# New ranks in a planned kernel, with diagonal blocks and conversion sums moved to DMA (gated attention and a low-rank mixer)

## Chip, cores, metric

One core of one Trainium2 chip. The metric is the device time of one execution, in microseconds; the median of several is quoted.

## The reference, cut

```python
# attention: B=4, H=8, S=768, D=48; a gate a = a_re + i a_im with |a| clipped to 0.999
S_re, S_im = a * S   (complex);  S_re += k v^T;  y_t = q_t . S_re        # step by step in t
x = y as (B, S, 384)
h = x^T @ U @ V              # mixes ALL 768 positions of a batch, rank 32
u = x + h^T
out = u + relu(u @ w_ch1) @ w_ch2        # 384 -> 1536 -> 384
```

The kernel cuts each sequence into chunks of 128 positions: 6 chunks a batch, 24 in all, numbered through. `x^T @ U` needs all six chunks of a batch, so the mixer of batch 0 can't start before chunk 5 has left attention.

## The kernel before

It doesn't write its instructions in program order. Every operation is declared with an engine, an estimated duration and a **rank**, and a list scheduler (`Plan.order`) simulates the engines and emits, on each free engine, the ready operation of the lowest rank. The result is one fixed order for each engine; on the chip each engine walks through its list and waits where an input is missing.

```python
# cut: the heart of Plan.order
while free[e] <= now and ready[e]:
    r = heapq.heappop(ready[e])        # lowest rank among the READY ones
    n = r[1]
    if not fits(n):                    # no free buffer: try the next
        kept.append(r)
        continue
    ...
    out.append(n)
    free[e] = now + ops[n][1]          # estimated duration
```

```python
# cut: ranks of the kernel before (i = chunk, lo = first chunk of a group of two)
#   gates lo-1.6   angles lo-1.5   prep i-0.8   levels i   rest i+0.5
#   conversion: w1 0.6 + 0.8*p (p = 0..5), UV 3.2, w2 7.0 + 0.2*f   mixing (up, down): 100+m
def single(p, rank, to, o, pieces):    # cut: float64 -> float32, seven VectorE instructions a piece
    ...
    DVE(two, rank, lambda: nc.vector.scalar_tensor_tensor(out=xf(), in0=lo(), scalar=2.0 ** -52, in1=xf(), op0=OP.mult, op1=OP.mult), ...)
    DVE(two, rank, lambda: nc.vector.tensor_tensor(out=o, in0=o, in1=xf(), op=OP.add), reads=[cx], writes=[to])

# cut: the second half of a group's gates ("turns"), with ScalarE's trigonometric table loaded
switch(R2, "trig_and_small")
ACT sign; ACT arctan; DVE y = ...; ACT y = y/pi + 1/4
for i in group:                        # the phase is summed from chunk to chunk
    if not first of its batch:
        POOL(... nc.gpsimd.dma_start(out=of(y, i)[0:1], in_=fo(i - 1)[CH - 1:CH], accum_op=OP.add) ...)
    PE ph = prefix^T @ y;  ACT F = round(ph);  DVE F = ph - F
ACT abs; ACT sin; ACT sin              # cs, which prep of both chunks needs

# cut: chain(i), the rest of it
for j in range(CH // BLK):
    ACT(0.4, RR, lambda js=js: nc.scalar.copy(out=get(*ATi)[js, :, js], in_=get(*DGi)[js]), [DGi], [ATi + (("d", js.start),)])
```

## Time and profile before

| | before |
|---|---|
| median of 3 runs | 816.72 us (814.86 to 817.06) |
| span of the profiled run | 815.9 us |
| first `mixed` matmul (end of stage 1) | 185.5 us |
| TensorE busy | 743.5 us |

Read it as two stages. Up to the first `mixed`, only attention can run. After it, the mixer's matmuls (`up`, `down`) fill every gap of TensorE. **Stage 1** goes from 10 us (the first matmul) to the first `mixed`; its length minus TensorE's busy time in it is its **idle**, and the same for stage 2. For the kernel before, the windows at this cut (columns: stretch, length, PE, PEld, DVE, ACT, POOL, clock, DMA share, GB/s) are:

```profile
10.00:185.50 175.50, 120.42 (x2032) 93.43 (x2032) 142.54 (x202) 132.31 (x261) 4.87 (x6) 0.75 0.40 98
185.50:815.90 630.40, 623.07 (x7480) 471.27 (x7480) 301.76 (x408) 330.57 (x713) 43.13 (x54) 0.99 0.15 34
```

So stage 1 has 175.5 - 120.4 = 55.1 us idle, and stage 2 has 7.3, the last store.

### The profile page before, as it was taken

The numbers are of one execution on the slowest core, as the hardware profiler recorded it, in microseconds if no ns is written. First come the engines' busy times: TensorE is split into PE (matmuls) and PEld (weight loads), VectorE is DVE, ScalarE is ACT, GpSimd is POOL, SyncE is SP. The second block draws the span as 40 slices with busy tenths as digits, with TensorE's granted clock in tenths as the row PEclk, the third lists the DMA queues.
The fourth block names the chain that finished last, engine by engine and source line by source line (L and its number), as shares of the span: only waits on it lengthen the run. The fifth ranks groups of instructions, "written<-read, shape, count | busy, mean of one in ns | idle before, by whom it ended". The sixth has DMA issues, their size and how long they took to land.

```text
span 815.9 us, 21434 instructions
## 1 busy us (share of the span) xinstructions
PE 743.5 (91%) x9512; PEld 564.7 (69%) x9512; DVE 447.2 (55%) x622; ACT 468.7 (57%) x983; POOL 55.9 (7%) x89
## 2 busy tenths in 40 slices
PE   2556786779999999999999999999999999999996
PEld 1445565657877877787787688687786867677683
DVE  3899687888978594747657585455451210110100
ACT  6886676877876787878587677745341312021120
POOL 3000000000101010010001010010000000000000
PEclk9767666898999999999999999999999999999999
DMA  7435323344022221403122240200000000000000
GB/s 186 113 91 132 90 41 99 60 117 107 13 59 51 50 53 38 90 12 58 42 47 47 47 90 2 49 22 1 21 12 10 11 10 10 10 10 19 10 10 20
DMA packets 131532, 40.11 MB, mean 49 GB/s; under 512 B 127088, under 2 KB 127984, under 8 KB 131440
## 3 DMA queue, kind: packets, MB, share of 16 engines
q1 hardware_dynamic: 129264, 33.99, 19.0%
q0 software_dynamic: 2176, 4.75, 1.7%
q8 instruction: 75, 1.23, 0.6%
q14 instruction: 17, 0.14, 0.1%
HBM read 33.59 MB, written 4.72 MB: 47 GB/s over the span
## 4 chain that ended last, share of the span: by engine, by line
PE 82%; DVE 6%; ACT 5%; issue 3%; DMA 3%; POOL 0%; POOLq 0%; ACTq 0%; DVEq 0%
PE up L765 23%; PE down L776 22%; PE tr L551 5%; PE inner L585 5%; PE tot L467 4%; PE dk L695 3%; PE yT L681 3%; PE es ps L450 3%; PE ph L511 2%; PE yT L685 2%; PE mixed L747 2%; PE ks ps L667 2%; DVE QK L248 2%; PE corners L632 2%; DMA y<-F 1%
## 5 line engine op out<-in xcount | busy, mean ns | idle before, releaser
L765 PE MATMUL up<-uT,w 128*128 128x256 f32 x864 | 201.8, 384 | 0.0
L776 PE MATMUL down<-w,h 128*128 128x384 f32 x576 | 199.6, 489 | 0.0
L248 DVE TENSOR_TENSOR QK<-QK,T 96x1024 f32<-96x1024 f32 (+1 forms) x144 | 172.8, 1206 | 24.0 <-PE corners L632 16.7
L765 PEld LDWEIGHTS up<-uT,w 128*128 128x128 f32 x864 | 159.2, 190 | 23.9 <-issue 1.4
L776 PEld LDWEIGHTS down<-w,h 128*128 128x128 f32 x576 | 105.0, 190 | 60.0 <-issue 0.4
L245 ACT ACTIVATE h<-up 128x256 f32<-128x256 f32 x144 | 55.2, 383 | 147.6 <-PE up L765 146.7
L551 PE MATMUL tr<-ident,qkc 128*96 128x128 f32 x384 | 58.5, 298 | 11.8 <-DVE qkc L248 10.8
L585 PEld LDWEIGHTS inner<-QK 96*32 96x32 f32 x4608 | 48.2, 112 | 28.6 <-issue 18.1
L251 DVE TENSOR_TENSOR xo<-down,xo 128x384 f32<-128x384 f32 x24 | 13.4, 556 | 97.4 <-PE down L776 97.0
L554 ACT COPY QK<-tr 96x512 f32<-96x512 f32 x96 | 52.8, 582 | 23.6 <-PE tr L551 22.7
L585 PE MATMUL inner<-QK 96*32 96x16 f32 (+1 forms) x4608 | 55.6, 192 | 11.1 <-DVE QK L248 10.7
L551 PEld LDWEIGHTS tr<-ident,qkc 128*96 128x96 f32 x384 | 44.5, 136 | 25.4 <-DVE qkc L248 13.6
L248 DVE TENSOR_TENSOR qkc<-qk,cs 128x768 f32<-128x768 f32 x48 | 44.1, 956 | 28.4 <-PE tr L551 21.9
L251 DVE TENSOR_TENSOR xo<-mixed,xo 128x384 f32<-128x384 f32 x24 | 13.3, 556 | 81.7 <-PE mixed L747 80.8
L467 PEld LDWEIGHTS tot<-total,ll 128*96 128x96 f32 x384 | 39.7, 180 | 8.6 <-ACT ll L462 3.1
L467 PE MATMUL tot<-total,ll 128*96 128x63 f32 x384 | 40.8, 263 | 2.5 <-ACT ll L462 2.5
L623 ACT COPY AT<-DG 32x256 f32<-32x256 f32 x96 | 38.4, 400 | 6.9 <-DVE DG L592 5.6
L681 PE MATMUL yT<-AT,VP 128*64 128x128 f32 x384 | 41.3, 305 | 0.9 <-ACT AT L651 0.5
L450 PE MATMUL es ps<-l,mid 128*128 128x384 f32 x48 | 24.4, 635 | 19.4 <-DVE l L440 19.4
L782 POOL DMA_DIRECT2D out_dram<-xo x24 | 13.6, 565 | 333.3 <-DVE xo L251 325.9
L712 ACT COPY xo<-yr 128x384 f32<-128x384 f32 x24 | 11.4, 476 | 43.0 <-DMA out_dram<-xo 39.2
L514 DVE SCALAR_TENSOR_TENSOR F<-F,ph 128x384 f32<-128x384 f32 x24 | 13.3, 554 | 41.1 <-ACT F L245 41.1
(92 smaller groups left out, 972.2 us busy)
## 6 DMA issues: line engine op xcount, KB each, us to landing
ar<-in_a_re_dram SPq DMA_DIRECT2D x24, 192.0 KB, 3.2
ai<-in_a_im_dram SPq DMA_DIRECT2D x24, 192.0 KB, 3.5
qk<-in_q_dram SPq DMA_DIRECT2D x24, 192.0 KB, 3.1
qk<-in_k_dram SPq DMA_DIRECT2D x24, 192.0 KB, 3.5
VP<-in_v_dram SPq DMA_DIRECT2D x24, 192.0 KB, 2.8
raw<-in_moe_w_ch_dram SPq DMA_DIRECT2D x6, 768.0 KB, 5.4
raw<-in_moe_w_ch_dram SPq DMA_DIRECT2D x12, 384.0 KB, 3.9
out_dram<-xo POOLq DMA_DIRECT2D x24, 192.0 KB, 2.2
```

What stands on the lines that cost most here:

```text
L245: return nc.scalar.activation(out=o, in_=i, func=f, **kw)
L248: nc.vector.tensor_tensor(out=o, in0=a, in1=b, op=OP.mult)
L251: nc.vector.tensor_tensor(out=o, in0=a, in1=b, op=OP.add)
L450: PE(0.65, R1, lambda: nc.tensor.matmul(out=get(*ps), lhsT=mid, rhs=of(l, i), start=True, stop=True), [l, ("mid", 0)], [ps, ("sums", g, i)])
L467: nc.tensor.matmul(out=get(*ps)[0:D2, h, 0:NTOT], lhsT=get(*ll)[:, h].rearrange("p u d -> p (u d)"), rhs=total, start=True, stop=True)
L551: nc.tensor.transpose(out=get(*ps)[0:D2, j], in_=get(*qkc)[:, u, hh * HH + j].rearrange("p u d -> p (u d)"), identity=ident)
L554: ACT(c_act(HH * CH) - 0.05, R1, lambda u=u, hh=hh, ps=ps: nc.scalar.copy(out=get(*QK)[:, u, hh * HH:(hh + 1) * HH], in_=get(*ps)[0:D2]), ...
L585: nc.tensor.matmul(out=get(*ps)[js, h], lhsT=k_of(h)[:, js], rhs=part(q_of(h)[:, js], "p"), start=True, stop=True, tile_position=(0, j * BLK))
L623: ACT(0.4, RR, lambda js=js: nc.scalar.copy(out=get(*ATi)[js, :, js], in_=get(*DGi)[js]), [DGi], [ATi + (("d", js.start),)])
L681: nc.tensor.matmul(out=a[u * DP:(u + 1) * DP, p], lhsT=vv[:, h], rhs=get(*ATi)[:, h], start=True, stop=(c == 0), tile_position=(0, u * DP))
L765: nc.tensor.matmul(out=get(*ps), lhsT=w1[:, f, ff * 128:(ff + 1) * 128], rhs=get(*uT)[:, f], start=(f == 0), stop=(f == KD - 1))
L776: nc.tensor.matmul(out=get(*ps), lhsT=get(*h)[:, ff, cc * CH:(cc + 1) * CH], rhs=w2[:, ff], start=(ff == 0), stop=(ff == KF - 1))
```

## The change

Its intent: let VectorE and ScalarE do less in stage 1 (the last sum of each conversion and the placing of the diagonal blocks go to DMA), and let nothing unurgent stand in attention's way (ranks, with constants that look searched for). The diff, cut to its core:

```diff
+PARAM = {"gates": -0.48, "angles": -1.91, "prep": -2.39, "levels": -4.96, "rest": 1.63, "w1": 18.64, "w2": 32.63, "first": 6.42}
+    def urgency(kind, n):
+        if kind == "load":
+            return n - 20
+        if kind in ("small", "mixing"):
+            return n + (1000 if kind == "mixing" else -1000)
+        if kind in ("w1", "w2"):
+            return PARAM[kind] + 0.01 * n
+        return n + PARAM[kind] + (PARAM["first"] if n >= NCH else 0)
 ...
-        DVE(two, rank, lambda: nc.vector.tensor_tensor(out=o, in0=o, in1=xf(), op=OP.add), reads=[cx], writes=[to])
+        POOL(1.0, rank, lambda: nc.gpsimd.dma_start(out=o, in_=xf(), accum_op=OP.add), reads=[cx], writes=[to], late=4.0)
 ...
-            ACT(0.4, RR, lambda js=js: nc.scalar.copy(out=get(*ATi)[js, :, js], in_=get(*DGi)[js]), [DGi], ...)
+            SP(0.15, RR, lambda js=js: nc.sync.dma_start(out=get(*ATi)[js, :, js], in_=get(*DGi)[js]), [DGi], ...)
 ...
+    AT_ONCE = (0, 1, 2, 3)      # groups (chunks 0 to 5) whose sines come in their own session
+        waits = [waves]         # the others: in the next group's trigonometric session
```

Also: `cx` has two buffers instead of one, T six instead of five, VP three instead of four, `qkc` is halved, the loads have ranks of their own, the scaled phase has its own tile `z` (it was `y`), the sign of the gate is taken before the trigonometric session and no longer in it, one table load of the first group goes, and the plan multiplies TensorE's durations in the first batch by 1.3.

More of the change, by code (lines that the diff above doesn't have):

```diff
@@ L23, with __init__ @@
 BLK = 32
+PARAM = {"gates": -0.48, "angles": -1.91, "prep": -2.39, "levels": -4.96, "rest": 1.63, "w1": 18.64, "w2": 32.63, "first": 6.42}
 class Plan:
-    def __init__(self, lag):
-        self.lag = lag
+    def __init__(self, lag, urgency):
+        self.lag, self.urgency = lag, urgency
         self.ops, self.log, self.tag, self.bufs = [], {}, {}, {}
@@ L55, in order @@
         ops = self.ops
+        rank = [self.urgency(*o[3]) for o in ops]
         left = [len(o[5]) for o in ops]
@@ L83, in order @@
             if not left[n]:
-                heapq.heappush(ready[o[0]], (o[3], n))
+                heapq.heappush(ready[o[0]], (rank[n], n))
         while True:
@@ L116, in order @@
                         if not left[m]:
-                            heapq.heappush(ready[ops[m][0]], (ops[m][3], m))
+                            heapq.heappush(ready[ops[m][0]], (rank[m], m))
         assert len(out) == len(ops), "the plan is stuck"
@@ L178 @@
     singles = pool("singles")
-    plan = Plan(0.06)
+    def urgency(kind, n):
[6 more added lines that the diff above has]
+        return n + PARAM[kind] + (PARAM["first"] if n >= NCH else 0)
+    plan = Plan(0.06, urgency)
     makers, T, pools = {}, {}, {}
@@ L218, in c_dma, with PE @@
         return n * 512 / 170e3
-    def PE(*a, **kw):
-        plan.add("PE", *a, **kw)
+    def PE(cost, rank, *a, **kw):
+        plan.add("PE", cost * (1.3 if rank[0] not in ("small", "mixing") and rank[1] < NCH else 1.0), rank, *a, **kw)
     def ACT(*a, **kw):
@@ L271 @@
     total = singles.tile([128, NTOT], FP, name="total")
+    F = singles.tile([128, GC, DM], FP, name="F")
     w1 = singles.tile([128, KD, FF], FP, name="w1")
@@ L288 @@
     AT, DG, VP = [], [], []
-    for n in range(4):
+    for n in range(3):
         VP.append(singles.tile([128, H, DP], FP, name="VP%d" % n))
@@ L298, in constants @@
     def constants():
-        SP(0.4, -7.5, lambda: nc.sync.dma_start(out=prefix, in_=spans[:, PRE * CH:(PRE + 1) * CH]), writes=[("prefix", 0)])
-        SP(0.6, -2.4, lambda: nc.sync.dma_start(out=mask, in_=masks), writes=[("mask", 0)])
+        SP(0.4, ("load", 0.1), lambda: nc.sync.dma_start(out=prefix, in_=spans[:, PRE * CH:(PRE + 1) * CH]), writes=[("prefix", 0)])
+        SP(0.6, ("load", 1.2), lambda: nc.sync.dma_start(out=mask, in_=masks), writes=[("mask", 0)])
         e = prefix.rearrange("p (b t) -> p b t", t=8)
-        POOL(0.5, -7, lambda: nc.gpsimd.tensor_tensor(
+        POOL(0.5, ("load", 0), lambda: nc.gpsimd.tensor_tensor(
             out=mid.rearrange("p (b t) -> p b t", t=8), in0=e[:, :, 3:4].to_broadcast([128, CH // 8, 8]), in1=e,
@@ L323, in totals @@
                     nc.gpsimd.tensor_tensor(out=to[:, 1:m], in0=ends[:, 1:m], in1=ends[:, 0:m - 1], op=OP.subtract)
-        POOL(2.5, -6, totals, reads=[("prefix", 0)], writes=[("total", 0)])
+        POOL(2.5, ("load", 1), totals, reads=[("prefix", 0)], writes=[("total", 0)])
         def pairs():
@@ L329, in pairs @@
                 nc.vector.tensor_tensor(out=mask[:, 5], in0=mask[:, 5], in1=mask[:, n], op=OP.bitwise_or)
-        DVE(0.5, -4, pairs, writes=[("mask", 0)])
+        DVE(0.5, ("load", 1), pairs, writes=[("mask", 0)])
     def load_a(g):
@@ L338, in load_a @@
             for i in range(lo, hi):
-                SP(c_dma(DM), lo - 8 if g == 0 else lo - 3, lambda nm=nm, src=src, i=i: nc.sync.dma_start(
+                SP(c_dma(DM), ("load", (0, 0.5, 3)[g] if g < 3 else lo + 3), lambda nm=nm, src=src, i=i: nc.sync.dma_start(
                     out=get(nm, g)[:, i - lo], in_=rows(src, i)), writes=[(nm, g, i)])
@@ L345, in load_qkv @@
         for u, src in enumerate((q, k)):
-            SP(c_dma(DM), i - 2.3, lambda u=u, src=src: nc.sync.dma_start(out=get("qk", i)[:, u], in_=rows(src, i)),
+            SP(c_dma(DM), ("load", (1.3, 2.5)[i] if i < 2 else i + 3.7), lambda u=u, src=src: nc.sync.dma_start(out=get("qk", i)[:, u], in_=rows(src, i)),
                writes=[("qk", i, u)])
-        SP(c_dma(DM), i - 2.0, lambda: nc.sync.dma_start(out=get("VP", i)[:, :, 0:D], in_=rows(v, i)), writes=[("VP", i)])
+        SP(c_dma(DM), ("load", (1.4, 2.6)[i] if i < 2 else i + 4), lambda: nc.sync.dma_start(out=get("VP", i)[:, :, 0:D], in_=rows(v, i)), writes=[("VP", i)])
     def single(p, rank, to, o, pieces):
@@ L359, in single @@
             for a, at in zip(pieces, ends):
-                SP(c_dma(a.shape[1]), rank - 1.5, lambda a=a, at=at: nc.sync.dma_start(out=o[:, at:at + a.shape[1]], in_=a),
+                SP(c_dma(a.shape[1]), ("load", 3.6 + p * 0.5), lambda a=a, at=at: nc.sync.dma_start(out=o[:, at:at + a.shape[1]], in_=a),
                    writes=[to])
@@ L363, in single @@
         buffer(("raw", p), "raw", 2, [128, WP, 2])
-        buffer(("cx", p), "cx", 1, [128, WP])
+        buffer(("cx", p), "cx", 2, [128, WP])
         for a, at in zip(pieces, ends):
-            SP(c_dma(2 * a.shape[1]), rank - 1.5, lambda a=a, at=at: nc.sync.dma_start(
+            SP(c_dma(2 * a.shape[1]), ("load", (1, 2, 3.5)[p] if p < 3 else 3.6 + p * 0.5), lambda a=a, at=at: nc.sync.dma_start(
                 out=get("raw", p)[:, at:at + a.shape[1]], in_=a.bitcast(U32).rearrange("p (m two) -> p m two", two=2)),
@@ L393, in weights @@
             for f in range(KD):
-                single(p, 0.6 + 0.8 * p, ("w1", f, h), w1[:, f, h:h + WP], [moe_w_ch1[f * 128:(f + 1) * 128, h:h + WP]])
+                single(p, ("w1", p), ("w1", f, h), w1[:, f, h:h + WP], [moe_w_ch1[f * 128:(f + 1) * 128, h:h + WP]])
                 p += 1
-        single(p, 3.2, ("UV", 0), UV, [moe_U[c * 128:(c + 1) * 128] for c in range(NCH)] +
+        single(p, ("w1", p), ("UV", 0), UV, [moe_U[c * 128:(c + 1) * 128] for c in range(NCH)] +
                [moe_V.rearrange("r (s m) -> (r s) m", m=m)])
@@ L399, in weights @@
         for n in range(NP):
-            SP(0.6, 3.2, lambda n=n: nc.sync.dma_start(out=V[n * R:(n + 1) * R].rearrange("r (s m) -> r s m", m=m),
+            SP(0.6, ("load", 7), lambda n=n: nc.sync.dma_start(out=V[n * R:(n + 1) * R].rearrange("r (s m) -> r s m", m=m),
                                                        in_=UV[:, NCH * R:]), reads=[("UV", 0)], writes=[("V", 0, n)])
         for f in range(0, KF, 2):
-            single(p, 7.0 + 0.2 * f, ("w2", f), w2[:, f:f + 2].rearrange("p f m -> p (f m)"),
+            single(p, ("w2", f), ("w2", f), w2[:, f:f + 2].rearrange("p f m -> p (f m)"),
                    [moe_w_ch2[e * 128:(e + 1) * 128] for e in (f, f + 1)])
@@ L412, in gates @@
         W = (hi - lo) * DM
-        R1, R2 = lo - 1.6, lo - 1.5
+        R1, R2 = ("gates", lo), ("angles", lo)
         ca, cd = c_act(W), c_dve(W)
-        x, y, l, n, ar, ai = names = [(nm, g) for nm in ("x", "y", "l", "n", "ar", "ai")]
-        for b in names[:4]:
-            buffer(b, "g" + b[0], 1, [128, GC * DM])
+        x, y, l, n, z, ar, ai = names = [(nm, g) for nm in ("x", "y", "l", "n", "z", "ar", "ai")]
         def t(b):
@@ L424, in of @@
             return get(*b)[:, (i - lo) * DM:(i - lo + 1) * DM]
-        ACT(ca, R1, lambda: act(t(x), t(ar), AF.Square), [ar], [x])
-        ACT(ca, R1, lambda: act(t(y), t(ai), AF.Square), [ai], [y])
-        DVE(cd, R1, lambda: add(t(x), t(x), t(y)), [y], [x])
-        DVE(c_one(W), R1, lambda: nc.vector.tensor_scalar(out=t(x), in0=t(x), scalar1=M2LO, scalar2=M2HI, op0=OP.max,
-                                                          op1=OP.min), [], [x])
-        switch(R1, "natural_log_exp_and_others")
@@ L432, in gates @@
-        ACT(ca, R1, lambda: act(t(n), t(ar), AF.Abs), [ar], [n])
-        table(ca, R1, lambda: act(t(l), t(x), AF.Ln), [x], [l])
-        table(ca, R1, lambda: act(t(x), t(l), AF.Exp, scale=0.5), [l], [x])
-        DVE(cd, R1, lambda: add(t(x), t(x), t(n)), [n], [x])
-        table(ca, R1, lambda: act(t(y), t(l), AF.Exp, scale=-0.5, bias=leps), [l], [y])
-        table(ca, R1, lambda: act(t(y), t(y), AF.Ln, bias=1.0), [], [y])
-        ACT(ca, R1, lambda: act(t(l), t(l), AF.Relu, scale=-0.5, bias=lmax), [], [l])
@@ L440, in gates, with magnitudes @@
-        DVE(cd, R1, lambda: nc.vector.scalar_tensor_tensor(out=t(l), in0=t(l), scalar=LNMAX, in1=t(y), op0=OP.subtract,
-                                                           op1=OP.add), [y], [l])
-        table(ca, R1, lambda: act(t(x), t(x), AF.Ln), [], [x])
-        table(ca, R1, lambda: act(t(x), t(x), AF.Exp, scale=-1.0), [], [x])
-        DVE(cd, R1, lambda: mul(t(x), t(x), t(ai)), [ai], [x])
+        def magnitudes():
+            for b in names[:4]:
+                buffer(b, "g" + b[0], 1, [128, GC * DM])
+            ACT(ca, R1, lambda: act(t(x), t(ar), AF.Square), [ar], [x])
+            ACT(ca, R1, lambda: act(t(y), t(ai), AF.Square), [ai], [y])
+            DVE(cd, R1, lambda: add(t(x), t(x), t(y)), [y], [x])
+            DVE(c_one(W), R1, lambda: nc.vector.tensor_scalar(out=t(x), in0=t(x), scalar1=M2LO, scalar2=M2HI, op0=OP.max,
+                                                              op1=OP.min), [], [x])
+            ACT(ca, R1, lambda: act(t(n), t(ar), AF.Abs), [ar], [n])
+            table(ca, R1, lambda: act(t(l), t(x), AF.Ln), [x], [l])
+            table(ca, R1, lambda: act(t(x), t(l), AF.Exp, scale=0.5), [l], [x])
+            DVE(cd, R1, lambda: add(t(x), t(x), t(n)), [n], [x])
+            table(ca, R1, lambda: act(t(y), t(l), AF.Exp, scale=-0.5, bias=leps), [l], [y])
+            table(ca, R1, lambda: act(t(y), t(y), AF.Ln, bias=1.0), [], [y])
+            ACT(ca, R1, lambda: act(t(l), t(l), AF.Relu, scale=-0.5, bias=lmax), [], [l])
+            DVE(cd, R1, lambda: nc.vector.scalar_tensor_tensor(out=t(l), in0=t(l), scalar=LNMAX, in1=t(y), op0=OP.subtract,
+                                                               op1=OP.add), [y], [l])
+            table(ca, R1, lambda: act(t(x), t(x), AF.Ln), [], [x])
+            table(ca, R1, lambda: act(t(x), t(x), AF.Exp, scale=-1.0), [], [x])
+            DVE(cd, R1, lambda: mul(t(x), t(x), t(ai)), [ai], [x])
+            ACT(ca, R1, lambda: act(t(n), t(ar), AF.Sign, bias=tiny), [ar], [n])
+            for i in range(lo, hi):
+                within(i)
@@ L458, in of_blocks @@
             psum(ps, "T", [128, H, 64])
-            buffer(tt, "T", 5, [D2, H * NTOT])
+            buffer(tt, "T", 6, [D2, H * NTOT])
             (ACT if i < NCH + GC else POOL)(
@@ L474, in of_blocks, with totals @@
                     T_of(i, n), get(*ps)[0:D2, :, FIRST[n]:FIRST[n] + CH // n], AF.Exp, scale=-1.0), [ps], [tt + (n,)])
+        def totals():
+            for i in range(lo, hi):
+                of_blocks(i)
         def turns():
-            switch(R2, "trig_and_small")
-            ACT(ca, R2, lambda: act(t(y), t(ar), AF.Sign, bias=tiny), [ar], [y])
+            buffer(z, "gz", 1, [128, GC * DM])
             table(ca, R2, lambda: act(t(x), t(x), AF.Arctan), [], [x])
-            DVE(cd, R2, lambda: nc.vector.scalar_tensor_tensor(out=t(y), in0=t(x), scalar=math.pi / 4, in1=t(y),
-                                                               op0=OP.subtract, op1=OP.mult), [x], [y])
@@ L483, in turns @@
-            ACT(ca, R2, lambda: act(t(y), t(y), AF.Identity, scale=1.0 / math.pi, bias=fourth), [], [y])
-            buffer(("F", g), "F", 2, [128, GC, DM])
+            DVE(cd, R2, lambda: nc.vector.scalar_tensor_tensor(out=t(z), in0=t(x), scalar=math.pi / 4, in1=t(n),
+                                                               op0=OP.subtract, op1=OP.mult), [x, n], [z])
+            ACT(ca, R2, lambda: act(t(z), t(z), AF.Identity, scale=1.0 / math.pi, bias=fourth), [], [z])
             for i in range(lo, hi):
@@ L486, in turns @@
                 angles(i)
-            cs = ("cs", g)
-            buffer(cs, "cs", 2, [128, GC, H, 2, D])
-            def halves(u):
-                return get(*cs).rearrange("p c h u d -> p (c h) u d")[:, 0:W // D, u]
-            f = ("F", g)
-            ft = lambda: get(*f).rearrange("p c m -> p (c m)")[:, 0:W]
-            ACT(ca, R2, lambda: act(t(n), ft(), AF.Abs), [f], [n])
-            table(ca, R2, lambda: act(halves(1), heads(ft()), AF.Sin, scale=2.0 * math.pi), [f], [cs + (1,)])
@@ L496, in turns @@
-            table(ca, R2, lambda: act(halves(0), heads(t(n)), AF.Sin, scale=-2.0 * math.pi, bias=quarter), [n], [cs + (0,)])
         def angles(i):
-            def fo(i):
-                return get("F", group_of(i))[:, i - GROUPS[group_of(i)][0]]
-            f = ("F", g, i)
-            yi = y + (i,)
+            fo = lambda i: F[:, i % GC]
+            f = ("F", i)
+            plan.buffer(f, "F", GC)
+            zi = z + (i,)
             if where(i)[1] > 0:
-                POOL(0.55, R2, lambda: nc.gpsimd.dma_start(out=of(y, i)[0:1], in_=fo(i - 1)[CH - 1:CH], accum_op=OP.add),
-                     [("F", group_of(i - 1), i - 1)], [yi], late=1.6)
+                POOL(0.55, R2, lambda: nc.gpsimd.dma_start(out=of(z, i)[0:1], in_=fo(i - 1)[CH - 1:CH], accum_op=OP.add),
+                     [("F", i - 1)], [zi], late=1.6)
@@ L509, in angles @@
             ps = ("ph", i)
             psum(ps, "T", [128, DM], [128, 512])
-            PE(0.65, R2, lambda: nc.tensor.matmul(out=get(*ps), lhsT=prefix, rhs=of(y, i), start=True, stop=True),
-               [yi, ("prefix", 0)], [ps])
+            PE(0.65, R2, lambda: nc.tensor.matmul(out=get(*ps), lhsT=prefix, rhs=of(z, i), start=True, stop=True),
+               [zi, ("prefix", 0)], [ps])
             ACT(c_act(DM), R2, lambda: act(fo(i), get(*ps), AF.Identity, scale=-1.0, bias=magic), [ps], [f])
@@ L515, in angles, with waves, half @@
                                                                       op0=OP.subtract, op1=OP.add), [ps], [f])
-        for i in range(lo, hi):
-            within(i)
-        if g == 0:
-            turns()
-            switch(R2, "natural_log_exp_and_others")
-        for i in range(lo, hi):
-            of_blocks(i)
-        if g > 0:
-            turns()
+        def waves():
+            cs = ("cs", g)
+            buffer(cs, "cs", 2, [128, GC, H, 2, D])
+            def half(u):
+                return get(*cs).rearrange("p c h u d -> p (c h) u d")[:, 0:W // D, u]
+            fs = [("F", i) for i in range(lo, hi)]
+            ft = heads(F.rearrange("p c m -> p (c m)")[:, lo % GC * DM:lo % GC * DM + W])
+            ACT(ca, R2, lambda: act(half(0), ft, AF.Abs), fs, [cs + (0,)])
+            table(ca, R2, lambda: act(half(1), ft, AF.Sin, scale=2.0 * math.pi), fs, [cs + (1,)])
+            table(ca, R2, lambda: act(half(0), half(0), AF.Sin, scale=-2.0 * math.pi, bias=quarter), [], [cs + (0,)])
+        return magnitudes, totals, turns, waves
     def T_of(i, n):
@@ L532, in prep @@
     def prep(i):
-        R1 = i - 0.8
+        R1 = "prep", i
         g = group_of(i)
-        qk, qkc, QK = ("qk", i), ("qkc", i), ("QK", i)
-        buffer(qkc, "qkc", 1, [128, 2, H, 2, D])
+        qk, QK = ("qk", i), ("QK", i)
         buffer(QK, "QK", 3, [D2, 2, H, CH])
@@ L541, in prep @@
                 [("es", i, u)], [qk + (u,)])
-            DVE(c_dve(2 * DM), R1, lambda u=u: mul(
-                get(*qkc)[:, u], get(*qk)[:, u].unsqueeze(2).to_broadcast([128, H, 2, D]), get("cs", g)[:, i - GROUPS[g][0]]),
-                [qk + (u,), ("cs", g)], [qkc + (u,)])
+            qkc = ("qkc", 2 * i + u)
+            buffer(qkc, "qkc", 1, [128, H, 2, D])
+            DVE(c_dve(2 * DM), R1, lambda u=u, qkc=qkc: mul(
+                get(*qkc), get(*qk)[:, u].unsqueeze(2).to_broadcast([128, H, 2, D]), get("cs", g)[:, i - GROUPS[g][0]]),
+                [qk + (u,), ("cs", g)], [qkc])
             for hh in range(2):
@@ L547, in prep, with turn @@
                 psum(ps, "T", [128, HH, CH])
-                def turn(u=u, hh=hh, ps=ps):
+                def turn(qkc=qkc, hh=hh, ps=ps):
                     for j in range(HH):
-                        nc.tensor.transpose(out=get(*ps)[0:D2, j], in_=get(*qkc)[:, u, hh * HH + j].rearrange("p u d -> p (u d)"),
+                        nc.tensor.transpose(out=get(*ps)[0:D2, j], in_=get(*qkc)[:, hh * HH + j].rearrange("p u d -> p (u d)"),
                                             identity=ident)
-                PE(0.44, R1, turn, [qkc + (u,)], [ps])
+                PE(0.44, R1, turn, [qkc], [ps])
                 ACT(c_act(HH * CH) - 0.05, R1, lambda u=u, hh=hh, ps=ps: nc.scalar.copy(
@@ L560, in chain @@
         c = where(i)[1]
-        RL, RR = i, i + 0.5
+        RL, RR = ("levels", i), ("rest", i)
         QK, DGi, ATi, VPi = ("QK", i), ("DG", i), ("AT", i), ("VP", i)
@@ L622, in chain @@
             js = slice(j * BLK, (j + 1) * BLK)
-            ACT(0.4, RR, lambda js=js: nc.scalar.copy(out=get(*ATi)[js, :, js], in_=get(*DGi)[js]), [DGi], [ATi + (("d", js.start),)])
+            SP(0.15, RR, lambda js=js: nc.sync.dma_start(out=get(*ATi)[js, :, js], in_=get(*DGi)[js]), [DGi],
+               [ATi + (("d", js.start),)])
         grow(RR, 16)
@@ L720, in mixer @@
         N = MC * CH
-        R0, RM = -5.0, 100.0 + m
+        R0, RM = ("small", m), ("mixing", m)
         r = ("r", b)
@@ L794, with chunks @@
     weights()
-    for g in range(NG):
-        load_a(g)
-        gates(g)
+    exps, trigs = "natural_log_exp_and_others", "trig_and_small"
+    def chunks(g):
         for i in range(*GROUPS[g]):
@@ L804 @@
                     mixer(m)
+    waits, later, done = [], [], 0
+    for g in range(NG):
+        load_a(g)
+        magnitudes, totals, turns, waves = gates(g)
+        rank = "gates", GROUPS[g][0]
+        switch(rank, exps)
+        for f in later:
+            f()
+        later = []
+        magnitudes()
+        if g:
+            totals()
+        else:
+            later = [totals]
+        switch(rank, trigs)
+        turns()
+        for f in waits:
+            f()
+        waits = [waves]
+        if g in AT_ONCE:
+            waves()
+            waits = []
+        ready = g + 1 - len(waits) - (g == 0)
+        while done < ready:
+            chunks(done)
+            done += 1
+    for f in waits:
+        f()
+    chunks(NG - 1)
     for n in plan.order():
```

## The prediction

> **What bounds the kernel now.** I read the page's busy tenths first, then windows, the groups by form, the chain of waits and the waits. The tenths show two stages:
>
> ```profile
> PE   2556786779999999999999999999999999999996
> DVE  3899687888978594747657585455451210110100
> ACT  6886676877876787878587677745341312021120
> PEclk9767666898999999999999999999999999999999
> ```
>
> From slice 10 on (204 us) TensorE is at 9 in every slice and its clock is full. Before that it is at 2 to 8, with a clock of 0.6 to 0.7, while VectorE and ScalarE are at 6 to 9. The cause is in the program: `rank` of a batch sums over all six chunks of it, so no mixing (`up`, `down`: 401 us of TensorE, the two costliest rows) can begin until chunk 5 has left attention. The chain view has the first `mixed` at 185.51 us. Until then nothing exists that could fill TensorE. I cut there:
>
> ```profile
> 0.00:186.00 186.00, 120.91 (x2033) 93.92 (x2034) 145.86 (x216) 138.66 (x272) 12.79 (x35) 0.77 0.42 102
> 10.00:186.00 176.00, 120.91 (x2033) 93.92 (x2034) 143.01 (x203) 132.81 (x262) 4.87 (x6) 0.75 0.40 98
> 186.00:816.00 630.00, 622.58 (x7480) 470.78 (x7479) 301.30 (x407) 330.07 (x712) 43.13 (x54) 0.99 0.15 34
> ```
>
> The columns are stretch, length, PE, PEld, DVE, ACT, POOL, clock, DMA share, GB/s. After 186 us, 7.4 us of TensorE are idle, nearly all of it the last store. So **stage 2 can't shrink except by less TensorE work, and the change removes no matmul**. Before 186 us, between the first matmul (10 us) and the first mixing, DVE is busy 143.0/176 = 81% and ACT 132.8/176 = 75%, neither full: stage 1 is bound by a chain that hops between four engines, with DVE nearest to a bound. Multiplying the matmul counts of stage 1 by their mean durations between 230 and 680 us gives 95.8 us against 133.8 us as measured, so the same matmuls would need some 96 of the 176 us: about 80 us are idle or slow clock. That is all that can be won.
>
> Two things stand on stage 1's chain that need not be there. The first is the conversion of weights to single precision (tiles `cx` and `w`). Its share of DVE in the two stages, in the windows for tile `cx`, is:
>
> ```profile
> 0.00:186.00 186.00, 50.74 (x74) 0.77 0.42 102
> 186.00:816.00 630.00, 13.38 (x18) 0.99 0.15 34
> ```
>
> So 50.7 of 143.0 us of DVE in stage 1 are conversion, and parts of it stand in the chain:
>
> ```profile
> 49.57 0.48 DVE cx L379
> 50.08 0.97 DVE w L381
> 51.07 0.57 DVE cx L383
> 51.67 0.97 DVE cx L385
> 52.66 0.85 DVE w L387
> ```
>
> Summing such pieces of the chain over 10 to 186 us gives 11.9 us for conversion and 2.7 us for the copies AT<-DG of line 623. The second is the phase carried from chunk to chunk by an accumulating DMA:
>
> ```profile
> 73.29 4.34 issue
> 77.64 5.66 DMA y<-F
> ...
> 126.38 1.82 DMA y<-F
> ...
> 174.32 3.65 DMA y<-F
> ```
>
> These are 11.1 us of DMA and some issue time, which the change leaves.
>
> **What the Trainium skill says.** (1) "TensorE: Matmul & The Clock Gate", Part 1 (the HAM clock gate): the array is throttled by default, and activity releases it. The trace agrees: 0.75 in stage 1, 0.99 after; one `es ps` matmul lasts 893 ns before 186 us and 505 ns between 230 and 680 us. A denser stage 1 therefore gains a little twice. (2) "DMA: Bandwidth & Descriptors", SWDGE vs HWDGE vs iDMA: an accumulating DMA can only be issued from GpSimd, where descriptors are written by software; the section Anatomy of one DMA fits 2.0 us plus bytes/436e3. For a 384 KB last sum that is 2.9 us, an estimate from that page; the trace has only 1.5 KB accumulations, 1.9 to 5.7 us to landing. (3) "SBUF — State Buffer", Who interferes with whom: a VectorE instruction in a two-port mode can lock GpSimd out of the ports through which it writes descriptors. The trace does not separate this from other delay, but 5.7 us for 1.5 KB shows that carries are sometimes late.
>
> **The change part by part.**
>
> *Last sum by DMA.* Line 387 goes from DVE: 0.95 us for each of 12 pieces and 0.56 us for UV, 12.0 us in all, 9.1 of them in stage 1. Added are 13 DMAs of GpSimd, whose engine is 7% busy. They share a queue with the carries, so a carry may wait for one.
>
> *Urgencies.* Conversions had ranks 0.6 to 4.6 (w1), 3.2 (UV) and 7 to 9 (w2), among chunks 0 to 8, and so went ahead of attention. They now have 18.6 and 32.6: they come only where DVE has nothing else ready. Before the mixing, w1 and UV are still needed: a piece costs 4 x 0.556 + 2 x 0.953 = 4.1 us without its last sum, six cost 24.8, and UV 4 x 0.36 + 2 x 0.55 = 2.5. That is 27.3 us instead of 50.7: **23.4 us of DVE less in stage 1**. The w2 pieces that move to stage 2 find DVE there at 301/630 = 48%. The order within attention changes too: later batches get 6.42 more, so gates and prep of chunks 6 and 7, done in stage 1 until now, yield to the rest of chunk 5. That shortens stage 1, but leaves their matmuls (for gates 25.2 us over 8 chunks at full clock, so 3.1 us a chunk) to stage 2. It nets a few us at most.
>
> *Diagonal blocks by DMA.* Four ACT copies of 0.40 us per chunk go, 9.6 us in stage 1 (24 copies). Four SyncE transfers of 32 KB replace them. The qk loads of 192 KB land in 3.1 us, so I guess 2 to 3 us for these, against 1.6 us for four copies in series. It is one or two us more latency in a chain whose other half (two DVE multiplications of 1.2 us, two groups of products, four ACT copies) lasts longer, so it should be hidden.
>
> *Sines.* Up to chunk 5 they come at once, as now. One of 12 table loads before 186 us goes (the return to exponentials in the first group), 1.3 us. From chunk 6 on, the sines wait for the next group's session; this takes carries off stage 2's ACT, where TensorE is already full: nothing.
>
> *The sum, three ways.* (a) By the chain: 11.9 + 2.7 + 1.3 = 15.9 us off it; a new limiter usually stands close behind, so I count three quarters, 12 us. (b) By DVE at its present 81%: (143.0 - 23.4)/0.81 = 148 us instead of 176, so 28 us. (c) By ACT at its present 75%: (132.8 - 9.6 - 1.3)/0.755 = 161 us, so 15 us. As work is also reordered to bring chunk 5 forward, I choose between (b) and (c): **20 us off stage 1**, hence 816.7 - 20 = 796.7, and I say 796.
>
> **The rivals.** *The chain stays.* If stage 1 is held by latencies (carries, table sessions, TensorE at the low clock), DVE's freed time turns into idle time. For it: neither DVE nor ACT is full, and PE pieces are the largest part of stage 1's chain. Against it: nearly 12 us of conversion stand in the chain itself. It would give 803 to 812.
>
> *Weights too late.* With such low urgency, w1's halves or w2 may not be ready when mixing starts. There is one buffer for `h`, so `up` of the second pair waits for `down` of the first, which needs all of w2. A late w2 would leave TensorE with attention only. Against it: DVE has 176 - 92 = 84 us free of attention in stage 1, and w1 with UV need 27. It would cost 5 to 15 us: 800 to 810.
>
> *DMA latency becomes the wait.* Carries behind 384 KB accumulations, or diagonal blocks behind loads that block SyncE's queue (that queue waits for buffers up to 43 us at a time), could hold `yT`. Against it: loads are placed in the order in which buffers come free, and DG and AT are double. It would give 805 to 820.
>
> *More than that.* If the searched urgencies keep DVE above 85%, stage 1 falls to 140 us, and the whole to 780.
>
> **Range and chances.** Central 796. The low end, 780, is the last rival; the high end, 812, is the chain that stays, or weights too late on top of a small gain. A gain of over 2% needs less than 800.4, some 16 us; (b) passes this and (c) just misses. The constants look searched for rather than chosen, which speaks for a real gain: 0.62 faster, 0.35 within 2%, 0.03 slower, since stage 2 has no slack to lose except through late weights.
>
> **What would show it.** Right: the first `mixed` moves from 185.5 to about 165 us; DVE conversion before it falls to about 27 to 35 us; AT<-DG is gone from ACT; after the first `mixed` TensorE idles under 12 us in all; the clock in stage 1 is above 0.75. Wrong: the first `mixed` stays past 178 us with DVE idler (the chain held), TensorE waits for `w` or `cx` after it (late weights), or `yT` waits for AT's DMA.

## The result

The changed kernel took **806.09 us** (804.44 to 807.13, 4 runs) against 816.89 us (the three runs of the table above and one more); the ratio is 0.9866, 95% interval 0.9836 to 0.9897. A second, longer measurement gave 803.07 us against 815.13, ratio 0.9853 (0.9819 to 0.9886). A ratio is the mean time of one kernel's fast runs over that of the other's of the same rounds, so not quite the ratio of the medians. The gain is real and just under 1.5%: within my range, but below the 2% that I had thought likelier than not.

The tenths of the changed kernel, answering to the first fence of the prediction:

```profile
PE   2667777989999999999999999999999999999996
DVE  5888898972857658287935828666541010110100
ACT  6776867687677676777676677653331202011020
PEclk9998668799999999999999999999999999999999
```

Counted from 0, as in the prediction, TensorE is at 9 from slice 9 on in both kernels, but slices 7 and 8 have risen from 7 and 7 to 9 and 8, and a slice is 0.33 us shorter here. The windows at its own cut, the first `mixed` at 170.2 us:

```profile
10.00:170.20 160.20, 117.27 (x2027) 92.26 (x2026) 137.36 (x201) 117.28 (x230) 15.63 (x18) 0.84 0.65 142
170.20:802.60 632.40, 623.35 (x7486) 470.00 (x7486) 292.39 (x398) 307.33 (x645) 42.50 (x56) 1.00 0.18 37
```

Stage 1 is 15.3 us shorter: 12.2 us less idle (42.9 instead of 55.1) and 3.1 us less TensorE time. The work in it is the same: its matmul counts times their full-speed durations come to 94.4 us against 95.4. (Full speed is the kernel before between 230 and 680 us; a matmul's duration is here the busy time of its group divided by its count, less than the printed mean, since matmuls overlap.) Stage 2 is 2.0 us longer. That is the whole difference between the two profiled spans, 13.3 us.

So far this is as foretold. But the means are not. The conversion of weights (windows for tile `cx`, same cut; the columns here are DVE, POOL, clock, DMA share, GB/s):

```profile
10.00:170.20 160.20, 48.63 (x74) 10.84 (x12) 0.84 0.65 142
170.20:802.60 632.40, 2.62 (x4) 0.90 (x1) 1.00 0.18 37
```

I had expected 27 us of it on VectorE in stage 1. There are 48.6: nearly what there was before (50.3 at the like cut), though each piece is cheaper, because nearly all of w2 now stands *in* stage 1: its second stage has 2.6 us of conversion, where it had 13.8. And VectorE's busy time in stage 1 fell by only 5.2 us (142.5 to 137.4) while the stage shrank by 15.3. Something other than VectorE's load had given way.

### The profile page after: what moved, and what is told of

Its sections match the earlier page's. It is cut to its first block, busy times and chain, and to the rows that moved or that the text cites. A ratio compares the mean times of both kernels' runs of the same rounds, so it can differ in the third digit from the quotient of the medians.

```text
span 802.6 us, 21566 instructions
## 1 busy us (share of the span) xinstructions
PE 741.0 (92%) x9512; PEld 562.6 (70%) x9512; DVE 432.8 (54%) x609; ACT 431.0 (54%) x886; POOL 65.8 (8%) x101
## 4 chain that ended last, share of the span: by engine, by line
PE 83%; DVE 7%; ACT 4%; issue 3%; DMA 3%; POOL 0%; POOLq 0%; DVEq 0%
PE up L783 24%; PE down L794 23%; PE tr L568 6%; PE inner L602 5%; PE tot L488 4%; PE yT L699 3%; PE dk L713 3%; PE es ps L471 3%; DVE QK L263 2%; PE ph L523 2%; PE yT L703 2%; PE ks ps L685 2%; DMA w<-cx 2%; PE corners L650 2%; PE mixed L765 2%
## 5 line engine op out<-in xcount | busy, mean ns | idle before, releaser
L783 PE MATMUL up<-uT,w 128*128 128x256 f32 x864 | 198.6, 382 | 0.0
L263 DVE TENSOR_TENSOR QK<-QK,T 96x1024 f32<-96x1024 f32 x144 | 170.8, 1195 | 17.8 <-PE corner L665 11.2
L260 ACT ACTIVATE h<-up 128x256 f32<-128x256 f32 x144 | 55.1, 383 | 156.7 <-PE up L783 155.5
L568 PE MATMUL tr<-ident,qkc 128*96 128x128 f32 x384 | 62.6, 306 | 13.5 <-DVE qkc L263 11.9
L602 PEld LDWEIGHTS inner<-QK 96*32 96x32 f32 x4608 | 49.2, 115 | 32.2 <-issue 18.2
L568 PEld LDWEIGHTS tr<-ident,qkc 128*96 128x96 f32 x384 | 47.2, 141 | 26.7 <-DVE qkc L263 7.7
L263 DVE TENSOR_TENSOR qkc<-qk,cs 128x768 f32<-128x768 f32 x48 | 45.8, 954 | 28.3 <-PE tr L568 20.6
L488 PE MATMUL tot<-total,ll 128*96 128x63 f32 x384 | 42.8, 267 | 4.4 <-ACT ll L483 4.3
L699 PE MATMUL yT<-AT,VP 128*64 128x128 f32 x384 | 40.9, 298 | 0.9 <-ACT AT L669 0.9
L471 PE MATMUL es ps<-l,mid 128*128 128x384 f32 x48 | 23.4, 596 | 12.9 <-DVE l L458 12.9
L609 DVE COPY_PREDICATED DG<-mask,inner 128x128 f32<-128x128 int32 (+1 forms) x72 | 24.7, 342 | 19.1 <-PE inner L602 15.9
L257 ACT ACT_TABLE_LOAD x26 | 33.4, 1283 | 1.2 <-PEq L894 0.7
```

Source lines behind the costliest of these rows:

```text
L257: table(1.28, rank, lambda: nc.scalar.preload_act_table_set(name))
L260: return nc.scalar.activation(out=o, in_=i, func=f, **kw)
L263: nc.vector.tensor_tensor(out=o, in0=a, in1=b, op=OP.mult)
L471: PE(0.65, R1, lambda: nc.tensor.matmul(out=get(*ps), lhsT=mid, rhs=of(l, i), start=True, stop=True), [l, ("mid", 0)], [ps, ("sums", g, i)])
L488: nc.tensor.matmul(out=get(*ps)[0:D2, h, 0:NTOT], lhsT=get(*ll)[:, h].rearrange("p u d -> p (u d)"), rhs=total, start=True, stop=True)
L568: nc.tensor.transpose(out=get(*ps)[0:D2, j], in_=get(*qkc)[:, hh * HH + j].rearrange("p u d -> p (u d)"), identity=ident)
```

## The experiments

All in one table (times from one profiled run each, ratios from all runs; "work" is stage 1's matmuls at full-speed durations). ScalarE has to load one table of functions for exponentials and another for sines; a *session* is the stretch from one such load to the next. "trig" is the length of its fourth trigonometric session, that of chunks 4 and 5:

| run | ratio (95%) | stage 1 | idle 1 | DVE 1 | ACT 1 | work | trig | stage 2 | idle 2 |
|---|---|---|---|---|---|---|---|---|---|
| before | 1 | 175.5 | 55.1 | 142.5 | 132.3 | 95.4 | 25.6 | 630.4 | 7.3 |
| changed | 0.9866 (0.9836-0.9897) | 160.2 | 42.9 | 137.4 | 117.3 | 94.4 | 19.3 | 632.4 | 9.1 |
| changed, again | 0.9853 (0.9819-0.9886) | 157.2 | 44.4 | 138.6 | 118.0 | 94.4 | 19.3 | 632.1 | 8.6 |
| a5: w2 after chunk 5 | 0.9923 (0.9866-0.9980) | 158.4 | 42.7 | 120.1 | 110.4 | 92.8 | 18.4 | 641.6 | 12.7 |
| a1: sums on DVE | 0.9899 (0.9849-0.9948) | 163.7 | 46.9 | 145.8 | 119.4 | 94.4 | 18.4 | 633.5 | 10.6 |
| a2: diagonal on ACT | 0.9956 (0.9895-1.0017) | 163.1 | 46.7 | 142.0 | 129.0 | 94.0 | 20.6 | 633.0 | 8.4 |
| a12: both back | 0.9913 (0.9873-0.9952) | 165.1 | 49.2 | 147.5 | 129.9 | 95.2 | 19.1 | 633.8 | 9.6 |
| a3: old ranks | 1.0032 (0.9969-1.0095) | 175.1 | 51.6 | 144.8 | 126.2 | 97.2 | 23.4 | 629.2 | 9.3 |
| a3b: old, attention only | 1.0004 (0.9956-1.0053) | 180.0 | 48.8 | 144.9 | 126.6 | 97.2 | 24.1 | 629.5 | 9.5 |
| a3c: old, weights only | 0.9955 (0.9908-1.0002) | 167.5 | 49.8 | 137.4 | 106.2 | 89.3 | 21.3 | 638.8 | 11.0 |
| a7: constants shifted | 0.9880 (0.9845-0.9915) | 160.1 | 43.9 | 137.9 | 118.0 | 94.0 | 19.7 | 635.1 | 10.4 |
| a4: all sines at once | 0.9892 (0.9851-0.9933) | 162.2 | 42.8 | 137.0 | 115.2 | 94.0 | 19.0 | 633.4 | 10.1 |
| a6: no carry (wrong result) | 0.9815 (0.9775-0.9856) | 149.6 | 40.8 | 133.6 | 109.1 | 92.8 | 13.3 | 639.6 | 11.0 |
| a8: carry by matmul | 0.9931 (0.9902-0.9961) | 163.5 | 40.9 | 143.0 | 122.2 | not comparable | 17.7 | 632.7 | 10.9 |

One profile is a blunt tool: the two "changed" lines are the same program, and their stage 1 differs by 3.0 us. I read nothing into differences of that size.

**Theories.** D: stage 1 is bound by VectorE's load (my way (b)). A: by ScalarE's load (way (c)). O: by the order in which each engine takes its work, along the chain from one group's session to the next; low-ranked conversions only fill gaps. S, a form of O: the chain runs through ScalarE's table sessions, each waiting for the phase carried from chunk to chunk.

### a5: w2 really kept out of stage 1

```diff
-        DVE(one, rank, ... reads=[raw], writes=[cx])              # first instruction of each w2 piece
+        DVE(one, rank, ... reads=[raw, ("xo", 5)], writes=[cx])   # declared after chain(5)
```

> The changed kernel with the conversion of w2 kept out of stage 1 by a true dependence: its first instruction reads the output of chunk 5. VectorE's conversion before the first mixing then falls from 49 to about 27 us, which my prediction had taken for what the new urgencies do by themselves. Theory D: stage 1 shortens by 20/0.86, the first mixing comes at about 148 us and the time is 782 to 788, ratio 0.96. Theory O: fillers are free, the first mixing stays within 4 us of 170 and the time is 803 to 810, or longer by 5 to 15 us if TensorE then waits for w2.

Measured 809.47 us, correct. The windows, all work and then tile `cx`:

```profile
10.00:168.40 158.40, 115.69 (x2017) 91.25 (x2017) 120.08 (x173) 110.41 (x219) 10.16 (x12) 0.84 0.52 114
168.40:810.00 641.60, 628.88 (x7498) 471.46 (x7496) 312.84 (x427) 315.76 (x658) 48.46 (x61) 0.99 0.21 44
```
```profile
10.00:168.40 158.40, 30.30 (x47) 6.32 (x7) 0.84 0.52 114
168.40:810.00 641.60, 21.66 (x31) 5.63 (x6) 0.99 0.21 44
```

VectorE lost 17.3 us of stage 1, from 137.4 to 120.1, and stage 1 lost 1.8, no more than two runs of one program differ; its idle stayed at 42.7 us. This is what my prediction had taken for the effect of the low rank, done by force, and it is worth nothing. **Theory D is refuted.** Stage 2 grew by 9.2 us instead: 3.7 us more idle and 5.5 us more TensorE time (1.6 us are matmuls left over from stage 1, 94.4 - 92.8 in the table; the recorded clock is 0.83 in its first 10 us against 1.00 in the changed kernel).

### a1, a2, a12: the DMA parts undone

```diff
a1, a12: -POOL(1.0, rank, lambda: nc.gpsimd.dma_start(out=o, in_=xf(), accum_op=OP.add), ...)
         +DVE(two, rank, lambda: nc.vector.tensor_tensor(out=o, in0=o, in1=xf(), op=OP.add), ...)
a2, a12: -SP(0.15, RR, lambda js=js: nc.sync.dma_start(out=get(*ATi)[js, :, js], ...), ...)
         +ACT(0.4, RR, lambda js=js: nc.scalar.copy(out=get(*ATi)[js, :, js], ...), ...)
```

> The changed kernel with the last sum of each conversion back on VectorE. Theory D (VectorE's load bounds stage 1, which it fills to 86%): 11 of 13 sums, about 10.5 us, come back into stage 1, so the first mixing moves from 170 us to about 181 and the time is about 816, ratio to before 1.00. Rival O (order bounds stage 1; conversions only fill gaps and cost nothing): the sums go into other gaps, first mixing within 3 us of 170, time 803 to 808, ratio 0.985 to 0.99.

> The changed kernel with the diagonal blocks copied by ScalarE again. ScalarE's busy time in stage 1 should rise by 24 x 0.40 = 9.6 us. Theories D and O both: ScalarE is only 73% busy there, so 0 to 3 us longer, ratio 0.986 to 0.990. Rival A (ScalarE's load bounds stage 1, since it fell by 15 us just as stage 1 did): first mixing about 180 us, time 815, ratio 0.998.

> The changed kernel with both DMA parts undone: last sums on VectorE, diagonal blocks on ScalarE; ranks, late sines and buffers as changed. If order alone carries the gain and both engines have room for the work, ratio 0.985 to 0.992. If the two parts add as they did one by one (0.9899 and 0.9956 against 0.9866), ratio about 0.999. VectorE's busy time in stage 1 should be about 146 us and ScalarE's about 128 us either way.

a1: 808.13 us. The sums came back (8.4 us of VectorE in stage 1), but D's 11 us did not: the first `mixed` came at 173.7 us, 3.5 later, just over the 3 that O allowed. a2: 812.71 us, with a wide spread (807.84 to 816.13); ScalarE's load rose by 11.7 us and stage 1 by 2.9, so theory A's 180 us did not come. Its time is worse than O allowed and its stage 1 is not, so I leave its size open (the profiled run was the fastest of its four). a12 takes both DMA parts away and keeps everything else: VectorE and ScalarE carry as much as before (147.5 and 129.9 us), and still the ratio to before is 0.9913, outside 1. **Ranks, late sines and buffers, without either DMA part, give 0.9%** of the 1.3 to 1.5%, and the two DMA parts together some 0.5%, which is not clear of the noise: the intervals overlap (a12's begins at 0.9873, the changed kernel's end at 0.9886 and 0.9897). Stage 1's idle points the same way: 55.1, then 49.2 without the DMA parts, then 42.9 to 44.4 with the DMA parts.

### a3, a3b, a3c: the ranks undone

```diff
a3, a3b: -"gates": -0.48, "angles": -1.91, "prep": -2.39, "levels": -4.96, "rest": 1.63, "first": 6.42
         +"gates": -1.6, "angles": -1.5, "prep": -0.8, "levels": 0.0, "rest": 0.5, "first": 0.0
a3, a3c: -return PARAM[kind] + 0.01 * n
         +return (0.6 + 0.8 * n if n < 6 else 3.2) if kind == "w1" else 7.0 + 0.2 * n
```

> The changed kernel (both DMA parts, late sines, buffers) with the old ranks for attention's five kinds of work and for the weights. Theory O: the gain lies in the order, so nearly all of it goes: about 814 to 818, ratio 0.997 to 1.00, VectorE in stage 1 back to about 81%. Theory D: what counts is the work that VectorE has in stage 1; under the old ranks part of w2 waits until stage 2, so the time stays at 803 to 808, ratio 0.985 to 0.99.

> The changed kernel with the old ranks of attention alone (gates, angles, prep, levels, rest, nothing extra for later batches); the weights keep their new, low ranks. Theory O1 (the gain is in the order within attention): nearly all of it goes, as with both undone, ratio 0.998 to 1.005, first mixing about 183 us. Rival O2 (the gain is that conversions no longer go ahead of attention): most of it stays, ratio 0.985 to 0.992, first mixing about 172 us.

> The changed kernel with the old ranks of the weights alone (0.6 to 4.6, 3.2, 7 to 9); attention keeps its new ones. The mirror of the run with attention's old ranks: O1 expects 0.985 to 0.992 and a first mixing within 4 us of 170; O2 expects 0.997 to 1.004 and about 183 us.

816.96, 816.98 and 814.09 us. With attention's old ranks the whole gain goes, although both DMA parts, the late sines and the buffers are still in: so these don't give the gain without the ranks. That is O1's ratio, but a3b's first `mixed` came at 190.0 us, later than O1's 183 (the profiled run was the slowest of its four). a3c fits neither: its ratio is 0.9955 where O1 allowed 0.992, its first `mixed` comes at 177.5 where O1 allowed 174 and O2 expected 183, and its interval lies just above those of the changed kernel. So the weights' ranks matter too. With them undone, stage 1 is 7.3 us longer (again in the slowest run of four) though VectorE is busy in it exactly as long as in the changed kernel, 137.4 us, and stage 2 is 6.4 us longer, having less work done ahead (89.3 us instead of 94.4). The two groups of ranks don't add up: undoing either loses most of the gain.

What the order does can be seen in ScalarE's list. This is the timeline of ScalarE in the session of chunks 4 and 5 in the kernel before (start, duration, instruction; in brackets what it waited for):

```profile
114.61 1.28 ACT L242 ACT_TABLE_LOAD   x1
...
118.78 0.83 ACT L245 ACTIVATE x<-x 128x768 f32<-128x768 f32 x1
121.06 0.59 ACT L689 COPY yTs<-yT 128x512 f32<-128x512 f32 x1 [1.45 <-PE yT L685]
121.54 0.81 ACT L623 COPY AT<-DG 32x256 f32<-32x256 f32 x2
124.66 0.48 ACT L712 COPY xo<-yr 128x384 f32<-128x384 f32 x1 [2.30 <-PE yr L710]
125.16 0.94 ACT L245 ACTIVATE y<-y,fourth 128x768 f32<-128x768 f32 x1
...
140.17 1.28 ACT L242 ACT_TABLE_LOAD   x1
```

The phase `y` was ready for ScalarE at 120.6 us (VectorE wrote it from 119.64 on, for 0.96 us). ScalarE scaled it at 125.16, because the *rest* of an earlier chunk (`yTs`, `AT`, `xo`) stood ahead in its list and was itself waiting. That is 4.5 us in which the carry, and with it everything behind the session, stood still. The chain view of the kernel before runs through exactly these leftovers into the phase (start, us, what):

```profile
121.01 2.73 PE dk L695 x16
123.74 0.89 PE yr L710 x4
124.66 0.48 ACT xo L712
125.16 0.94 ACT y L245
```

The rest's `dk` has 9.8 us of stage 1's chain in the kernel before and none in the changed one. There the session reads:

```profile
111.50 1.28 ACT L257 ACT_TABLE_LOAD   x1
112.79 0.84 ACT L260 ACTIVATE x<-x 128x768 f32<-128x768 f32 x1
...
115.04 0.94 ACT L260 ACTIVATE z<-z,fourth 128x768 f32<-128x768 f32 x1
...
130.81 1.28 ACT L257 ACT_TABLE_LOAD   x1
```

VectorE wrote `z` from 113.89 on, and ScalarE took it 0.2 us after it was done (leftovers, `AT<-corners`, stood ahead of it here too, but without waiting). The session lasts 19.3 us instead of 25.6; 2.9 of these 6.3 us were lost before the arctangent (118.78 and 112.79), where the sign also stood, which the new code takes earlier. The session isn't all of the gain: of the 15.3 us of stage 1 it has 6.3, it starts 3.1 us sooner, and from its end to the first `mixed` it takes 39.4 us instead of 45.3. In the table it lasts 23.4 us or more with attention's old ranks and 21.3 or less with the new ones.

a3 and a3b hide a second effect, so their loss is not the ranks' alone. Their plan puts a conversion's 384 KB accumulation just ahead of a carry in GpSimd's queue. The waits of TensorE in a3b have the cost (total, times, longest):

```profile
PE ph L523 <- DMA z<-F: 6.9, 6, 3.7
```

In the changed kernel the line reads:

```profile
PE ph L523 <- DMA z<-F: 1.5, 1, 1.5
```

In a12, which has no such accumulations, it reads 4.2, 3 times, longest 1.6. So of a3b's 6.9 us some 3 may be the third rival of my prediction, a carry behind an accumulation (one is issued at 119.96 us, the carry at 121.79); the changed kernel keeps the two apart in the first batch. That is less than the 11 to 12 us that a3b loses by the ratios.

### a7, a4: a mere reshuffle, and the late sines

```diff
a7: +PARAM = {"gates": -0.9, "angles": -1.5, "prep": -2.8, "levels": -4.5, "rest": 2.0, ..., "first": 6.0}
a4: -AT_ONCE = (0, 1, 2, 3)
    +AT_ONCE = tuple(range(NG))
```

> The changed kernel with its rank constants shifted by 0.35 to 0.46 each, gates -0.9, angles -1.5, prep -2.8, levels -4.5, rest 2.0, later batches 6.0: same ordering of the kinds, none of the engines' work changed. It measures how far a mere reshuffle of the same work moves the time. If reshuffles cost little, ratio 0.984 to 0.990; if the constants are a searched optimum, so that any shift loses 2 to 6 us, ratio 0.989 to 0.994, and then the 2 to 7 us that undoing single parts cost can't be put down to the engines' load.

> The changed kernel with the sines of every group at once, none left to the next session. My prediction said that late sines from chunk 6 on gain nothing, as TensorE is full there: ratio within 0.004 of the changed kernel's, 0.983 to 0.991. Rival: with sines at once, chunks 6 and 7 need only their own group's session, and the carry stands in ScalarE's order again; stage 2 then has several us more idle of TensorE, ratio about 0.995.

> The changed kernel unaltered, for a closer interval and for comparison with the other runs of this call on the same chip. Ratio 0.984 to 0.990.

a7: 806.20 us, a4: 805.81 us. Shifting all constants by about 0.4 costs 0 to 3 us by the medians and keeps the stages: in this one shift, the gain belongs to the sequence of the kinds of work, not to the second decimal. The late sines make no difference that can be told apart (0.9892 against 0.9853, intervals overlapping, stage 2 633.4 against 632.1 us).

### a6, a8: the carry

```diff
a6: -POOL(0.55, R2, lambda: nc.gpsimd.dma_start(out=of(z, i)[0:1], in_=fo(i - 1)[CH - 1:CH], accum_op=OP.add), ...)   # wrong on purpose
a8: +PE(0.65, R2, lambda: nc.tensor.matmul(out=get(*ps), lhsT=last, rhs=fo(i - 1), start=False, stop=True), [("F", i - 1), ...], [ps])
    # first batch only, in place of the DMA; last[127, :] = 1, all else 0
```

> Wrong result on purpose: the changed kernel without the accumulating DMA that carries the phase from chunk to chunk (20 of them, 5 for the first batch). Theory S (stage 1 is held by the chain of ScalarE's table sessions, each of which waits for the carry before its sines and so before the next exponentials): three sessions of two chunks lose 2 to 6 us each, so the first mixing comes at 158 to 164 us, ratio about 0.975. Rival: the carry is hidden behind other work of the session, first mixing within 3 us of 170, ratio 0.984 to 0.990.

> Correct result: in the first batch the phase is carried by a second matmul into the same accumulator (a matrix whose last row is ones times the chunk before), in place of the accumulating DMA; later batches as changed. Theory S: stage 1 loses most of what the run without any carry lost, first mixing at 160 to 165 us, but stage 2 gives back as there (less attention done ahead), so 1 to 5 us net gain on the changed kernel, ratio 0.981 to 0.986. Rival: TensorE's extra 5 matmuls and the reshuffle eat it, ratio 0.986 to 0.990.

a6 took 801.77 us (relative error 0.13, as intended). Its windows:

```profile
10.00:159.60 149.60, 108.75 (x2017) 86.10 (x2015) 133.57 (x196) 109.07 (x217) 10.10 (x11) 0.74 0.67 146
159.60:799.20 639.60, 628.65 (x7498) 473.01 (x7497) 296.98 (x403) 314.00 (x658) 32.67 (x42) 0.99 0.18 38
```

Without the carry, the session of chunks 4 and 5 lasts 13.3 us, the first `mixed` comes at 159.6 and stage 1 is 10.6 us shorter. The three sessions that wait for a carry are 3.3, 4.9 and 6.0 us shorter than in the changed kernel (2.2, 4.8 and 6.0 against its second profile). The engines also do less in this shorter stage, but that doesn't explain it: a5 has the same work (92.8 us), about the same load of ScalarE (110.4 us) and less of VectorE, and its stage 1 lasts 158.4 us. **Stage 1 is held by this chain: theory S.** But 7.2 us came back in stage 2 (5.3 of TensorE time, 2.0 idle), and by the ratios the time fell by only 3 to 4 us, with intervals that overlap: the ratio of 0.975 that S gave wasn't reached. The run starts its mixing with 1.6 us less work done ahead and a lower recorded clock (0.80 and 0.86 in its first 20 us, against 1.00 in the changed kernel).

a8, a correct kernel, was meant to harvest this, and missed: 809.97 us, slower than the changed kernel. Its three sessions are 2.1, 2.7 and 1.6 us shorter than the changed kernel's, less than in a6. So the DMA is only part of what the carry costs. The rest I put down to the dependence itself (chunk 5's phase still waits for chunk 4's matmul, ScalarE and VectorE), which no run isolates. And the gain was lost behind the sessions: from the end of the last to the first `mixed` it took 43.5 us instead of 39.4, so `mixed` came at 173.5 where S had 160 to 165. None of these kernels that is correct beats the changed one.

## Why the prediction was right or wrong

Range right, odds wrong: 0.62 on a gain over 2%, and it was 1.3 to 1.5%. Stage 1 shrank by 15.3 us (18.3 in the second profile) where I said 20, but not by the means that I counted, so even this nearness is in part luck. The measured time lies where my first rival, "the chain stays", put it (803 to 812), and its chain of carries and table sessions is what held stage 1; only, the new order shortened that chain, and the first `mixed` didn't stay past 178.

- **Stage 2 can't shrink**: right, 632.4 and 632.1 us against 630.4. TensorE idles 9.1 us in it, under the 12 that I gave.
- **"They come only where DVE has nothing else ready ... 23.4 us of DVE less in stage 1"**: the step that failed. A list scheduler leaves no engine idle while anything is ready, so a low rank doesn't postpone work; with VectorE idle in 19% of stage 1 it drew w2 *forward*. Conversion there stayed at 48.6 us, where I had 27.3. What the low rank is worth lies in when a conversion runs: a3c.
- **"The order within attention changes too ... It nets a few us at most"**: the other failure, the same one seen from the other side. Undoing attention's ranks alone (a3b) lost the whole gain.
- **Way (b), VectorE at 81%: 28 us.** Failed twice: the load fell by 5.2 us instead of 23.4, and a5 shows that more would not have mattered. **Way (c), ScalarE: 15 us**, came out at the measured size by accident: ScalarE fell by 15.0 us as stage 1 fell by 15.3, but putting its copies back moved stage 1 by only 2.9. High busy shares in a chain-bound stage are no rates by which work can be turned into time.
- **Way (a), the chain: 12 us**, had the right kind of argument and the wrong item, so that its 12 us is near the measured 11 to 12 is luck. In the changed kernel conversion holds 15.8 us of the chain (11.9 before), plus 13.9 us of waiting for its DMA, while VectorE's own idle for that DMA is 1.5 us. Fillers in the chain need not cost time: a5 took 18 us of them out of stage 1 and gained nothing. What left the path was the rest's work ahead of the phase (`dk`: 9.8 us to none) and most of the carries' DMA, which I said the change leaves: 11.1 us of the chain before, 3.6 after.
- **The diagonal blocks' DMA is hidden**: right; it lands in 2.3 us (I guessed 2 to 3), and TensorE has no wait for it in the list of waits.
- **An accumulation takes 2.9 us**: mis-sized, see below; harmless in this order, while in a3b's it may cost some 3 us.
- **Late sines: nothing**: not separable from nothing (a4).
- **First `mixed` at about 165**: 170.2 and 167.2. **Clock above 0.75**: 0.84 and 0.88. **Weights too late**: not seen; even in a5 TensorE's list of waits has none for a weight (in the 92 us after its first `mixed` it waited 2.1 us for `xo` and 0.8 for `uT`).
- **Misread lines**: in the tenths that I showed, the clock before slice 10 runs from 0.6 to 0.9, not to 0.7, and TensorE is at 9 in slice 9 already; the carry's landing starts at 1.8 us, not 1.9 (the chain shows 1.82). The "mean durations" behind the 95.8 us are busy time divided by count. None of this moves the sum.

What stays open: the shares of the two DMA parts (together 0.5%, within the noise), and which of the five ranks of attention does it. All were undone at once; that the rest should yield to the phase is read from the timelines and the chain, not isolated. Nor did any run undo the buffers, the loads' ranks or the earlier sign by themselves: a3b shows that they give nothing under attention's old ranks, not that they give nothing under the new ones.

## What to carry to other kernels

In a stage bound by a chain across in-order engines, ask what stands ahead of the critical instruction in its engine's list, not how busy the engine is: here a session in which the phase no longer stood behind waiting leftovers of earlier chunks lasted 19.3 us instead of 25.6, while taking 17.3 us of work off the busiest engine gave nothing. A low priority in such a list scheduler fills gaps and may bring work forward; only a dependence postpones it. And before counting a shorter first stage as gain, check what it leaves undone for the stage that is full: without the carry, 7.2 of 10.6 us came back.

## What the Trainium skill lacked or had wrong

- "DMA: Bandwidth & Descriptors", Anatomy of one DMA: its fit (2.0 us plus bytes/436e3) gives 2.9 us for 384 KB. The accumulating DMA from SBUF to SBUF took 4.1 to 8.3 us to land, median 7.1 with UV, and 6.9 for w alone in the profile's list. I found no figure for accumulation there. From the changed kernel:

```profile
w<-cx POOLq DMA_DIRECT2D x12, 384.0 KB, 6.9
...
AT<-DG SPq DMA_DIRECT2D x96, 32.0 KB, 2.3
...
z<-F POOLq DMA_DIRECT2D x20, 1.5 KB, 1.9
```

- "ScalarE: Activation LUTs", What ACT_TABLE_LOAD costs: 1283 ns agrees exactly with the 26 loads of the changed kernel. The 1380 ns of drain that it adds for every switch isn't seen: in the changed kernel's session above, the activation before the load ends at 111.47 us, the load at 111.50 takes 1.28 us and the next activation starts at 112.79.
- "TensorE: Matmul & The Clock Gate", Part 1: activity is said to release the throttle, and so I expected the clock to follow density. The recorded mean clock of stage 1 didn't: 0.90 in a3, whose stage 1 was as long as before, and 0.74 in a6, whose stage was shortest, and the summed busy time of stage 1's matmul groups over their work at full speed was 1.39 (135.2/97.2) in a3 against 1.30 (121.0/92.8) in a6. The page itself warns, in its caveats on HAM traces, that these records have been unreliable; these runs agree with that.
